# Two linear-attention blocks on one core: other places on the load queue for eight of ten form loads of M

## The chip, the cores and the metric

The kernel runs on one core of a Trainium2 chip. The metric is device time in microseconds for one execution, as the median of several runs. Before the change it is 567.69 us (3 runs, 566.89 to 568.5).

## The reference

Two independent blocks, A and B, of linear attention stand side by side; their outputs are joined on the last axis. Each has 2048 tokens (S), width 640 (D), 32 heads of 20:

```
qkv = (x @ wqkv) -> q, k, v per head
phi(t) = where(t > 0, t + 1, exp(t)) + 1e-6
kv = sum over s of phi(k)[s] (x) v[s]      # 20 x 20 per head
z  = sum over s of phi(k)[s]
o  = (phi(q) @ kv) / (phi(q) . z + 1e-6)
out = concat_heads(o) @ wo
```

All in float32.

## The kernel before, in words

Every matrix product in float32 precision is made of three products of a rounded high part and a remainder (`h` and `l` at the end of a name): high by high, high by low, low by high. ScalarE rounds to the high part, VectorE subtracts to get the low part.

The work falls into two halves.

*The k half* (to about 280 us) goes through both blocks' tokens. It computes phi(k) and the 640 x 640 matrix of x^T phi(k) (`gacc`). From `gacc` and the weights of v the products kv are made, and from kv and `wo` the matrix M = diag(kv) wo of 640 x 640, so that the output is (phi(q) / denominator) M. In this half a planner (class `Plan`) orders the instructions: each step is a note with an engine, a cost, and the parts of tiles it reads and writes. The low parts of x^T are written to DRAM (`xd`, one buffer for each unit of 512 tokens) and so are the ten forms of block A's M (`fd`): sums and differences of M's blocks, from which the last product is made with fewer multiplications. Each form is a pair, high and low, of 128 x 640 (320 KB each; forms 6, 7 and 9 are 128 x 320).

*The q half* goes by units of 512 tokens, 0 to 3 of block A and 4 to 7 of block B. Unit u has five columns c of 128 features. `qmm` makes a column of q with 15 matmuls of 128 x 512 (L1015 to L1017): five row blocks k, three products each. The moving operands are `xqh` (rounded by ScalarE at L1053 from the raw load `xqs`) and `xql` (the low part, loaded from `xd`). For column 0 of units 0 and 1 the order differs: first the ten products with `xqh` (L1153, L1154), then the five with `xql` (L1159). `qphi` takes exponential and relu on ScalarE and joins them on VectorE; `qacc` sums the denominator; `split_acc`, `denmm` (the matmuls `psd`, L1193 and L1194), `recip` and `divide` finish it for unit 0 during unit 1. Then `outmm(0)` makes the output of unit 0 with the forms `fh`, `fl` (0 to 5) and `fm`, `fl` (6 to 9), L1313. It follows unit 1's columns. Its products read forms 0 and 1, then 2 and 3, then 4, 5 and 8, then 6, 7 and 9.

In the q half the order is written by hand: `at(slot, f, ...)` hangs a step on a slot, `("q", u, c, k)` after the matmuls of row block k, or `("o", u, s)` after step s of the output. Slots fix the order in which each engine and each queue gets its instructions; the engines run ahead of each other as far as their waits allow. The loads go out on SP's queue, M's stores of block B and the output on POOL's. SP's transfers take eight semaphores in turn (DMAHW0 to DMAHW7), and one that takes a semaphore anew waits until the transfer that had it before has landed: at most eight are under way.

The steps that the change touches:

- `form_load(b, i)` issues two loads on SP, for the high and the low part of form i (L1140).
- `load_xraw` loads the raw x^T of a unit, five loads of 256 KB (`xqs`, L1046), `load_xq` the low parts, five of 256 KB (`xql`, L1050). Unit 1's first raw load hangs on `("q", 0, 0, 1)`, the other four on `("q", 0, 2, 2)`, its `xql` on `("q", 0, 3, 3)` and after.
- `mmm2(1, i)` makes a third of block B's M: 16 small matmuls (`psm`, L615), four copies by ScalarE (`mev`, L1076). `store_m` issues two stores to `md` on POOL (L1082); six calls make twelve stores, of 60 or 40 rows of 640.
- `load_wo` loads a group's rows of `wo` in two pieces (L631), for the planner through `mmm` (a note with cost 0.14 on SP) and for block B through `load_o`.

Of the kernel before, what the change touches and what calls it, by code (L numbers as in the profile page):

```python
# [15 lines left out]
DH = 20  # L16
# [61 lines left out]
class Plan:  # L78
# [9 lines left out]
    def note(self, engine, n, fn, w, r, ahead=None, dma=None, late=None, by=None, due=None, safe=0.0, lat=0.0):  # L88
        base = self.RATE.get(engine)
        j = Job(engine, base[0] + base[1] * n if base else n, fn, ahead, dma)  # L90
        for part, writes in [(p, True) for p in w] + [(p, False) for p in r]:
            sp = part.space
            if sp.where is not None and sp not in j.spaces:
                j.spaces.append(sp)
            for lo, hi, other, wrote in sp.uses:
                if lo < part.hi and part.lo < hi and (writes or wrote) and other is not j:
                    j.deps.add(other)
            if writes:
                sp.uses = [u for u in sp.uses if not (part.lo <= u[0] and u[1] <= part.hi and u[2] is not j)]
            sp.uses.append((part.lo, part.hi, j, writes))  # L100
        for d in j.deps:
            d.nexts.append(j)
        for sp in j.spaces:
            sp.left += 1
        if engine == "PE":
            j.ideal = self.pe_at
            self.pe_at += j.cost
        j.late = self.pe_at + (25.0 if late is None else late)
        if by is not None:
            j.late = self.pe_at + by  # L110
        j.by, j.set, j.safe, j.lat = by, due, safe, (LAT if due is None else 1.9) + lat
        self.jobs.append(j)
        return j
# [105 lines left out]
def tile_linear_attn_pair(ctx: ExitStack, tc: tile.TileContext, ins, out: bass.AP):  # L219
    nc = tc.nc  # L220
# [60 lines left out]
    note = plan.note  # L281
# [329 lines left out]
    def m_products(o, i, wo, hs):  # L611

        for p in (0, 64):
            for j in range(2):
                nc.tensor.matmul(o[p // 64][j * 64:j * 64 + 64, :HF],  # L615
                                 kvt[p:p + 64, 2 * i + j], wo[j][p:p + 64, hs], start=True, stop=True)

    def m_rows(b, i, a):

        rows = md[b].rearrange("(d h) n -> d h n", h=H)  # L620
        out = []
        for j in range(2):
            h0, nh = GROUPS[2 * i + j]
            n = nh // 2
            out.append((rows[:, h0 + a * n:h0 + a * n + n, :], slice(j * 64, j * 64 + DH * n)))
        return out

    def load_wo(eng, to, b, g):
        h0, nh = GROUPS[g]
        for p, row in ((0, h0 * DH), (64, (h0 + nh) * DH - 64)):  # L630
            eng.dma_start(to[p:p + 64], ins[b]["wo"][row:row + 64, :])  # L631

    def kvmm(k):
        ws = []
# [13 lines left out]
    def mmm(i):  # L648
        n = gn[0] - (3 if i % 2 else 4)
        ks = ((3, 4, 5)[n % 3], (3, 4, 5)[(n + 1) % 3], 6, 7)  # L650
        wo, m = ([Space(n, D, ANY) for _ in range(2)] for n in ("wo", "mev"))
        for j in range(2):
            note("SP", 0.14, lambda j=j: load_wo(nc.sync, wo[j].all.f, 0, 2 * i + j), [wo[j].all], [], ahead=14.0, dma=1.0)

        def products():
            for h in range(2):
                o = [BK[k].open("psm") for k in ks[2 * h:2 * h + 2]]
                m_products(o, i, [x.all.f for x in wo], slice(h * HF, h * HF + HF))

        note("PE", 1.3, products, [BK[k].all for k in ks], [x.all for x in wo] + [KVT.all])  # L660
        for h in range(2):
            hs = slice(h * HF, h * HF + HF)
            for a in range(2):
                k = ks[2 * h + a]
                note("ACT", HF, lambda a=a, k=k, hs=hs: act(m[a].all.f[:, hs], BK[k].tile[:, :HF], AF.Copy), [m[a][hs]],
                     [BK[k].all])
        for a in range(2):
            for j, (rows, part) in enumerate(m_rows(0, i, a)):
                w = 4 * i + 2 * a + j
                note("SP", 0.07, lambda a=a, rows=rows, part=part: nc.sync.dma_start(rows, m[a].all.f[part]),  # L670
                     [mdv[w:w + 1]], [m[a].all], dma=0.5)
# [87 lines left out]
    a, z, x = jh[0][0:P], jl[0][0:P], jr[0][0:P]  # L759
# [127 lines left out]
    for p in range(4, NPB):  # L887
        i, h = divmod(p - 2, 2)
# [9 lines left out]
    for p in range(NPB + 1, NP):  # L898
        if p == NPB + 1:
            fl = kvs  # L900
        else:
            i, h = divmod(p - NPB - 2, 2)
            gready(NG + i)
            fl = filled(NG + i, h, p in (NPB + 2, NP - 1))
        for (q, n), i in place.items():
            if q == p - NPB:
                fl.setdefault(n, []).append((mmm, i))
        kpair(p, fl)
        if p == NPB + 4:
            zsums(0)  # L910
        if p == NPB + 5:
            m_forms()
# [8 lines left out]
    j = note("HOST", 0.0, swap, [gate.all], [])  # L921
# [50 lines left out]
    for g, (h0, nh) in enumerate(GROUPS):  # L972
        cols = NC * DH * nh
        w = Space("wv", cols, (BD,))
# [46 lines left out]
    def at(slot, f, *a):  # L1021
        todo.setdefault(slot, []).append((f, a))
# [34 lines left out]
    def load_o(b, g):  # L1057
        tag = ("dsh0", "dsl0", "dsh1", "dsl1", "dah1", "dal1")[g]
        o = q2[0].tile([P, D], F32, name="wo", tag=tag, bufs=1)
        load_wo(nc.sync, o, b, g)  # L1060
        wot[b, g] = o
# [309 lines left out]
            at(a, form_split, b, i)  # L1371
            at(s, form_store, b, i)

    for i in range(6):
        at((("q", 0, 2, 1), ("q", 0, 2, 4), ("q", 0, 3, 1), ("q", 1, 0, 0), ("q", 1, 0, 2), ("q", 1, 1, 0))[i],
           form_load, 0, i)
    for i in range(6, 10):
        at(("q", 1, i - 5, 4) if i < 9 else ("q", 1, 4, 0), form_load, 0, i)

    for g in range(NGR):  # L1380
        at(("q", 0, 0, 0), load_o, 1, g)
# [1 line left out]
    for i in range(3):  # L1383
        at((("q", 0, 3, 1), ("q", 0, 4, 0), ("q", 0, 4, 4))[i], mmm2, 1, i)
        for h in range(2):
            at((("q", 0, 3, 3), ("q", 0, 3, 4), ("q", 0, 4, 2), ("q", 0, 4, 3), ("q", 1, 0, 1), ("q", 1, 0, 3))[2 * i + h],
               store_m, nc.gpsimd)

    for c, a in ((0, ("q", 1, 4, 1)), (2, ("q", 1, 4, 1)), (4, ("q", 2, 0, 3)), (1, ("q", 4, 0, 2)), (3, ("q", 4, 0, 2))):
# [11 lines left out]
    h = NG - 1  # L1401
# [26 lines left out]
    for v in range(1, NU):  # L1428
        w, u = v - 1, v + 1
# [8 lines left out]
        else:  # L1438
            a = (5, 6, 7, 8, 8, 10, 11) if v == 1 else (2, 3, 5, 6, 7, 9, 11)
# [75 lines left out]
```

## Time and profile before

| What | Before |
|---|---|
| median of 3 runs | 567.69 us (566.89 to 568.5) |
| the profiled execution | 569.47 us |
| its span, first to last instruction | 567.7 us |
| TensorE busy (PE) | 557.9 us, 98% |
| VectorE (DVE) | 414.3 us, 73% |
| ScalarE (ACT) | 351.5 us, 62% |
| POOL | 74.6 us, 13% |
| moved by DMA | 119.60 MB, mean 211 GB/s |
| mean granted TensorE clock | 0.994 |

Busy times are unions of the instructions' spans. Matmuls are pipelined, so that one that takes 0.39 us starts 0.23 us after the one before. Where rows name an idle time in brackets, the arrow points to what ended it. Times within the span count from its first instruction. The execution's own time is 1.77 us longer than the span.

### The profile page before, as it was taken

What the parts mean: (1) busy time and instruction counts of PE and PEld (TensorE: products, weight loads), DVE (VectorE), ACT (ScalarE), POOL (GpSimd) and SP (SyncE); (2) the same over time, 40 slices, a digit from 0 to 9 for tenths busy, and PEclk for the clock granted to TensorE, in tenths of its full rate; (3) what the DMA queues carried; (4) which work ended last, traced back from release to release, by engine and by line L of the source; (5) the groups of instructions that cost most, each with busy time, mean ns of one, the idle gap of its engine ahead of it and who ended that gap; (6) DMA issues with size and microseconds to landing.
All of it is one profiled execution on the core that took longest, in us unless ns stands there. A gap on an engine that the chain in (4) does not pass through costs nothing.

```text
span 567.7 us, 9238 instructions
## 1 busy us (share of the span) xinstructions
PE 557.9 (98%) x3368; PEld 501.2 (88%) x3368; DVE 414.3 (73%) x657; ACT 351.5 (62%) x644; POOL 74.6 (13%) x127
## 2 busy tenths in 40 slices
PE   8999999999999999999999799999999999999997
PEld 6999999989998899998885589898989989898997
DVE  7788687589987668887632499967788686767792
ACT  6777475574768647676227268775767666665551
POOL 1210111111113001111215003110012201001010
PEclk9999999999999999999999799999999999999999
DMA  8994765849869577897999965763363997122022
GB/s 313 377 259 117 184 166 114 270 110 312 257 136 268 185 191 225 240 273 212 353 282 326 373 236 164 272 218 120 107 241 124 346 389 262 48 75 92 1 94 92
DMA packets 69509, 119.60 MB, mean 211 GB/s; under 512 B 7320, under 2 KB 30776, under 8 KB 69464
## 3 DMA queue, kind: packets, MB, share of 16 engines
q1 hardware_dynamic: 59576, 90.39, 48.0%
q0 software_dynamic: 9600, 28.23, 18.0%
q8 instruction: 26, 0.43, 0.3%
q10 hardware_dynamic: 288, 0.39, 0.3%
q14 instruction: 19, 0.16, 0.1%
HBM read 72.44 MB, written 36.07 MB: 191 GB/s over the span
## 4 chain that ended last, share of the span: by engine, by line
PE 93%; DMA 4%; DVE 2%; issue 0%; ACT 0%; SPq 0%; DVEq 0%; ACTq 0%
PE psg L547 19%; PE pa L1313 12%; PE ka L315 10%; PE psq L1015 7%; PE psq L1016 7%; PE psq L1017 7%; PE pe L1313 6%; PE ke L315 5%; PE psr L547 5%; PE psk L812 4%; PE psb L1313 4%; PE kb L315 3%; DMA xql<-xd 2%; PE pskv L602 1%; DMA xqs<-in_A_xt 1%; PE psm L615 1%
## 5 line engine op out<-in xcount | busy, mean ns | idle before, releaser
L1015 PE MATMUL psq<-xqh,wh 128*128 128x512 f32 x190 | 74.8, 394 | 0.0
L1017 PE MATMUL psq<-xqh,wl 128*128 128x512 f32 x190 | 74.6, 393 | 0.0
L1016 PE MATMUL psq<-xql,wh 128*128 128x512 f32 x190 | 74.5, 392 | 0.0
L547 PE MATMUL psg<-pkh,xnl 128*128 128x512 f32 x160 | 63.0, 394 | 0.0
L547 PE MATMUL psg<-pkl,xnh 128*128 128x512 f32 x160 | 63.0, 393 | 0.0
L547 PE MATMUL psg<-pkh,xnh 128*128 128x512 f32 x160 | 62.4, 390 | 0.0
L1173 DVE SCALAR_TENSOR_TENSOR pq<-eq,rq 128x512 f32<-128x512 f32 x40 | 27.6, 691 | 44.2 <-ACT rq L1172 44.2
L1171 ACT ACTIVATE eq<-psq 128x512 f32<-128x512 f32 x40 | 24.0, 600 | 55.3 <-PE psq L1017 44.7
L493 ACT ACTIVATE kt<-ka 128x320 f32<-128x320 f32 x52 | 22.6, 435 | 56.3 <-PE ka L315 56.1
L410 POOL DMA_DIRECT2D zacc<-ek x32 | 26.2, 819 | 198.2 <-DVE ek L503 164.8
L1328 ACT ACTIVATE o<-pa 128x320 f32<-128x320 f32 x64 | 27.9, 438 | 26.2 <-PE pa L1313 25.5
L1015 PEld LDWEIGHTS psq<-xqh,wh 128*128 128x128 f32 x190 | 36.0, 189 | 8.3 <-issue 1.0
L1017 PEld LDWEIGHTS psq<-xqh,wl 128*128 128x128 f32 x190 | 36.0, 189 | 7.7
L1016 PEld LDWEIGHTS psq<-xql,wh 128*128 128x128 f32 x190 | 36.0, 189 | 7.3
L547 PEld LDWEIGHTS psg<-pkh,xnl 128*128 128x128 f32 x160 | 30.0, 188 | 6.5
L547 PEld LDWEIGHTS psg<-pkh,xnh 128*128 128x128 f32 x160 | 30.1, 188 | 4.9
L547 PEld LDWEIGHTS psg<-pkl,xnh 128*128 128x128 f32 x160 | 30.0, 188 | 4.8
L503 DVE SCALAR_TENSOR_TENSOR ek<-ek,kt 128x640 f32<-128x640 f32 x26 | 21.4, 821 | 16.2 <-ACT kt L502 16.2
L405 ACT ACTIVATE pkh<-ek,epst 128x640 fp32r<-128x640 f32 x32 | 26.4, 827 | 5.7 <-DVE ek L503 5.7
L406 DVE SCALAR_TENSOR_TENSOR pkl<-ek,pkh 128x640 fp32r<-128x640 f32 x32 | 26.2, 820 | 3.7 <-ACT pkh L405 3.7
L560 DVE TENSOR_TENSOR gacc<-psg,gacc 128x512 f32<-128x512 f32 x30 | 20.5, 688 | 11.6 <-PE psg L547 11.3
L309 DVE TENSOR_TENSOR xnl<-xns,xnh 128x640 fp32r<-128x640 f32 x32 | 25.6, 819 | 0.8 <-ACT xnh L306 0.8
(225 smaller groups left out, 1638.4 us busy)
## 6 DMA issues: line engine op xcount, KB each, us to landing
zacc<-ek POOLq DMA_DIRECT2D x32, 320.0 KB, 4.6
xql<-xd SPq DMA_DIRECT2D x40, 256.0 KB, 5.7
xd<-xl SPq DMA_DIRECT2D x29, 320.0 KB, 4.0
out<-o POOLq DMA_DIRECT2D x28, 320.0 KB, 3.9
xns<-in_A_x SPq DMA_DIRECT2D x16, 320.0 KB, 4.6
xts<-in_B_xt_tiles SPq DMA_DIRECT2D x16, 320.0 KB, 4.4
xns<-in_B_x SPq DMA_DIRECT2D x16, 320.0 KB, 5.8
xqs<-in_A_xt SPq DMA_DIRECT2D x20, 256.0 KB, 6.2
```

The source lines that it names most:

```text
L309: note("DVE", n, lambda: tt(lo.r, src.f, hi.f, op=OP.subtract), [lo], [src, hi], ahead=10.0)
L315: nc.tensor.matmul(o, a.r, w.r, start=start and k == i == 0, stop=k == n - 1 and i == 2, skip_group_check=True)
L405: note("ACT", n + 110, lambda: act(hi.r, p.f, AF.Identity, bias=epst), [hi], [p, K0.all], by=8.0)
L406: note("DVE", n, lambda: stt(lo.r, p.f, EPS, hi.f, op0=OP.add, op1=OP.subtract), [lo], [p, hi], by=9.0)
L410: note("POOL", 1.0, lambda: nc.gpsimd.dma_start(z.f, p.f, **kw), [z], [p], dma=1.0 if first else 1.86)
L547: nc.tensor.matmul(o[:, :n], a.r, w.r, start=j == 0 and q == 0, stop=j == 2 and q == 2, skip_group_check=True)
L1015: nc.tensor.matmul(o, whi, xhi, start=first, stop=False)
L1016: nc.tensor.matmul(o, whi, xlo, start=False, stop=False)
L1017: nc.tensor.matmul(o, wlo, xhi, start=False, stop=last)
L1173: nc.vector.scalar_tensor_tensor(pq[u][:, c, :], e, 1.0, r, op0=OP.min, op1=OP.add)
L1313: nc.tensor.matmul(ps, x, y, start=start and n == i == 0, stop=n == len(terms) - 1 and i == 2, skip_group_check=True)
L1328: copy = lambda x, y: nc.scalar.activation(x, y, AF.Copy)
```

## The change

Three edits. The loads of the ten forms of block A hang on other slots: forms 0 and 1 in unit 0 ahead of the four raw loads of unit 1's x^T, the other eight in unit 1, with 8 ahead of 6 and 7. The last four of the six `store_m` calls hang on slots of unit 1, where two did. `load_wo` cuts the group's rows out of `wo` first, and its note costs 0.07.

```
     def load_wo(eng, to, b, g):
         h0, nh = GROUPS[g]
-        for p, row in ((0, h0 * DH), (64, (h0 + nh) * DH - 64)):
-            eng.dma_start(to[p:p + 64], ins[b]["wo"][row:row + 64, :])
+        w = ins[b]["wo"][h0 * DH:(h0 + nh) * DH, :]
+        for p, row in ((0, 0), (64, nh * DH - 64)):
+            eng.dma_start(to[p:p + 64], w[row:row + 64, :])
...
-            note("SP", 0.14, lambda j=j: load_wo(nc.sync, wo[j].all.f, 0, 2 * i + j), [wo[j].all], [], ahead=14.0, dma=1.0)
+            note("SP", 0.07, lambda j=j: load_wo(nc.sync, wo[j].all.f, 0, 2 * i + j), [wo[j].all], [], ahead=14.0, dma=1.0)
...
-    for i in range(6):
-        at((("q", 0, 2, 1), ("q", 0, 2, 4), ("q", 0, 3, 1), ("q", 1, 0, 0), ("q", 1, 0, 2), ("q", 1, 1, 0))[i],
-           form_load, 0, i)
-    for i in range(6, 10):
-        at(("q", 1, i - 5, 4) if i < 9 else ("q", 1, 4, 0), form_load, 0, i)
+    for i, a in ((0, ("q", 0, 1, 0)), (1, ("q", 0, 1, 3)), (2, ("q", 1, 0, 1)), (3, ("q", 1, 0, 4)), (4, ("q", 1, 1, 1)),
+                 (5, ("q", 1, 1, 4)), (8, ("q", 1, 2, 1)), (6, ("q", 1, 2, 4)), (7, ("q", 1, 3, 1)), (9, ("q", 1, 4, 0))):
+        at(a, form_load, 0, i)
...
-            at((("q", 0, 3, 3), ("q", 0, 3, 4), ("q", 0, 4, 2), ("q", 0, 4, 3), ("q", 1, 0, 1), ("q", 1, 0, 3))[2 * i + h],
+            at((("q", 0, 4, 2), ("q", 0, 4, 3), ("q", 1, 0, 3), ("q", 1, 0, 4), ("q", 1, 1, 2), ("q", 1, 1, 3))[2 * i + h],
                store_m, nc.gpsimd)
```

After the change line numbers from `load_wo` to the table of the form loads are one higher, and behind that table one lower. On SP's queue, at the end of unit 0, there stand before (`xqs` is raw x^T, `fh` and `fl` a form's two parts with the form's number in `fdh01` and the like, `xql` the low part of x^T, here of unit 1):

```order
L1046 DMA xqs_3451<-in_A_xt 128x512
L1140 DMA fh_3501<-fdh00_100 128x640
L1140 DMA fl_3502<-fdl00_101 128x640
L1046 DMA xqs_3571<-in_A_xt 128x512
L1046 DMA xqs_3573<-in_A_xt 128x512
L1046 DMA xqs_3575<-in_A_xt 128x512
L1046 DMA xqs_3577<-in_A_xt 128x512
L1140 DMA fh_3585<-fdh01_102 128x640
L1140 DMA fl_3586<-fdl01_103 128x640
L1140 DMA fh_3602<-fdh02_104 128x640
L1140 DMA fl_3603<-fdl02_105 128x640
L1050 DMA xql_3633<-xd1_87 128x512
```

and after the change, in the same place:

```order
L1047 DMA xqs_3451<-in_A_xt 128x512
L1141 DMA fh_3476<-fdh00_100 128x640
L1141 DMA fl_3477<-fdl00_101 128x640
L1141 DMA fh_3489<-fdh01_102 128x640
L1141 DMA fl_3490<-fdl01_103 128x640
L1047 DMA xqs_3575<-in_A_xt 128x512
L1047 DMA xqs_3577<-in_A_xt 128x512
L1047 DMA xqs_3579<-in_A_xt 128x512
L1047 DMA xqs_3581<-in_A_xt 128x512
L1051 DMA xql_3627<-xd1_87 128x512
```

Form 1's pair moved ahead of four raw loads, and form 2's pair moved from ahead of the five `xql` to behind them. Further on SP's queue, in unit 1, the narrow forms stand before like this (`xqs` is now unit 2's; in `fm` lie forms 6 to 9):

```order
L1140 DMA fm_3790<-fdh06_114 128x320
L1140 DMA fm_3790<-fdl06_115 128x320
L1140 DMA fm_3790<-fdh07_116 128x320
L1140 DMA fm_3790<-fdl07_117 128x320
L1046 DMA xqs_3838<-in_A_xt 128x512
L1046 DMA xqs_3843<-in_A_xt 128x512
L1046 DMA xqs_3852<-in_A_xt 128x512
L1046 DMA xqs_3857<-in_A_xt 128x512
L1140 DMA fm_3790<-fdh08_112 128x640
L1140 DMA fm_3790<-fdl08_113 128x640
L1046 DMA xqs_3864<-in_A_xt 128x512
```

and after it like this:

```order
L1141 DMA fm_3807<-fdh08_112 128x640
L1141 DMA fm_3807<-fdl08_113 128x640
L1141 DMA fm_3807<-fdh06_114 128x320
L1141 DMA fm_3807<-fdl06_115 128x320
L1047 DMA xqs_3838<-in_A_xt 128x512
L1141 DMA fm_3807<-fdh07_116 128x320
L1141 DMA fm_3807<-fdl07_117 128x320
L1047 DMA xqs_3845<-in_A_xt 128x512
L1047 DMA xqs_3854<-in_A_xt 128x512
L1047 DMA xqs_3859<-in_A_xt 128x512
L1047 DMA xqs_3864<-in_A_xt 128x512
```

Form 8 moved ahead of 6 and 7 and of unit 2's raw loads; from form 9 on the queue is the same in both. On POOL's queue the stores of M (`md`) stand before between the sums of z (`zq`) and the stores of block B's forms (`fdh`, `fdl`):

```order
L688 DMA zq<-zd_95 32x4x5 x4
L1082 DMA md_99<-mev 20x3x640 x8
L1082 DMA md_99<-mev 20x2x640 x4
L1121 DMA fdh_4042<-fsh 128x640
L1121 DMA fdl_4043<-fsl 128x640
```

and after the change:

```order
L689 DMA zq<-zd_95 32x4x5 x4
L1083 DMA md_99<-mev 20x3x640 x8
L1083 DMA md_99<-mev 20x2x640 x4
L1122 DMA fdh_4042<-fsh 128x640
L1122 DMA fdl_4043<-fsl 128x640
```

Here nothing moved but the line numbers.

## Prediction

> **What bounds the kernel now.** First the chain that ended last, by engine (the page's part 4), then in order of time:
> ```profile
> PE 93%; DMA 4%; DVE 2%; issue 0%; ACT 0%; SPq 0%; DVEq 0%; ACTq 0%
> ...
> 300.51 6.17 DMA xqs<-in_A_xt
> 306.75 10.28 DMA xql<-xd
> ```
> TensorE carries 93% of the chain, and an edit of loads gains nothing there. Of the 4% of DMA the larger part, 16.5 us, is one place: the raw x^T of unit 1 and behind it the low parts of x^T (`xql`). So this place was read next. TensorE's timeline there (start, length, operation; in brackets the idle time before it):
> ```profile
> 310.89 0.39 PE L1154 MATMUL psq<-xqh,wl 128*128 128x512 f32 x1
> 314.76 0.63 PE L1159 MATMUL psq<-xql,wh 128*128 128x512 f32 x1 [3.48 <-DMA xql<-xd]
> 315.62 0.79 PE L1159 MATMUL psq<-xql,wh 128*128 128x512 f32 x1 [0.23 <-DMA xql<-xd]
> 317.07 1.93 PE L1159 MATMUL psq<-xql,wh 128*128 128x512 f32 x3 [0.66 <-DMA xql<-xd]
> 318.80 0.63 PE L1015 MATMUL psq<-xqh,wh 128*128 128x512 f32 x1
> ...
> 321.79 0.41 PE L1194 MATMUL psd<-ac,same 128*128 128x512 f32 x1
> 322.04 0.40 PE L1015 MATMUL psq<-xqh,wh 128*128 128x512 f32 x1
> 322.27 0.39 PE L1016 MATMUL psq<-xql,wh 128*128 128x512 f32 x1
> ```
> At full pace a matmul starts every 0.23 us (322.04 to 322.27). The first column of unit 1 does its ten products with `xqh` and then needs the five `xql` (L1159): it waits 3.48 us for the first and goes on as they land. Without a wait the column's end would be 310.89 + 6 x 0.23 = 312.27, and 322.04, fourteen matmuls on, would be 314.1: some 7.9 us are lost here. The windows of this stretch say how (after the length stand the busy times of TensorE, its weight loads, VectorE, ScalarE and POOL, then granted clock, DMA share, GB/s):
> ```profile
> 311.12:314.76 3.64, 0.16 (x2) 0.00 (x1) 2.13 (x3) 0.73 (x2) 1.16 (x2) 1.00 1.04 404
> 314.76:318.80 4.04, 3.15 (x5) 1.54 (x6) 0.00 (x0) 0.00 (x0) 0.00 (x0) 0.53 1.03 404
> 318.80:322.04 3.24, 3.24 (x10) 2.51 (x8) 0.69 (x1) 1.90 (x3) 0.00 (x0) 0.54 1.06 394
> ```
> The wire is full (share 1.03 and more) while TensorE waits, and after the wait TensorE runs at half clock until about 321.8. So two things are lost: time until the last `xql` lands, and then nine matmuls at half pace. What stands ahead of `xql` on SP's queue shows in its timeline:
> ```profile
> 296.85 0.54 SPq L1046 DMA_DIRECT2D xqs<-in_A_xt  x1
> 297.44 0.42 SPq L1140 DMA_DIRECT2D fh<-fdh  x1
> 297.91 0.43 SPq L1140 DMA_DIRECT2D fl<-fdl  x1
> 298.44 2.94 SPq L1046 DMA_DIRECT2D xqs<-in_A_xt  x4
> 301.43 0.42 SPq L1140 DMA_DIRECT2D fh<-fdh  x1
> 301.90 0.42 SPq L1140 DMA_DIRECT2D fl<-fdl  x1
> 302.43 0.48 SPq L1140 DMA_DIRECT2D fh<-fdh  x1
> 303.25 0.39 SPq L1140 DMA_DIRECT2D fl<-fdl  x1
> 303.89 5.38 SPq L1050 DMA_DIRECT2D xql<-xd  x5
> 310.42 0.32 SPq L1140 DMA_DIRECT2D fh<-fdh  x1
> 312.07 0.32 SPq L1140 DMA_DIRECT2D fl<-fdl  x1
> 313.71 0.32 SPq L1140 DMA_DIRECT2D fh<-fdh  x1
> 314.73 0.32 SPq L1140 DMA_DIRECT2D fl<-fdl  x1
> ...
> 318.18 0.32 SPq L1140 DMA_DIRECT2D fm<-fdl  x1
> ```
> SP's transfers use eight semaphores in turn, so from 310.42 on each issue tells that the transfer eight places before it has landed: form 1's `fl` at 310.42, form 2's `fh` at 312.07 and `fl` at 313.71, the first `xql` at 314.73 (TensorE starts at 314.76), the last at 318.18. They land in the order of the queue.
>
> **The change, part by part.** Form 2's pair (2 x 320 KB = 0.655 MB) leaves the place ahead of `xql`. What that is worth hangs on who else uses the wire. DMA queues of 310.4 to 313.7, when that pair landed, then q1 (SP) of 313.7 to 318.2, then the wire of 317 to 321, when SP had it alone:
> ```profile
> q1 hardware_dynamic: 408, 0.79, 61.8%
> q0 software_dynamic: 233, 0.55, 42.2%
> ...
> q1 hardware_dynamic: 722, 1.45, 82.9%
> ...
> DMA packets 715, 1.61 MB, mean 402 GB/s; under 512 B 79, under 2 KB 87, under 8 KB 715
> ```
> The other user is POOL (q0) with M's twelve stores. At the least, `xql` comes earlier by the pair's bytes on a free wire, 0.655 / 0.402 = 1.6 us; at the most by all the time between form 1's and form 2's landings, 313.71 - 310.42 = 3.3 us. SP's own rate up to the last `xql`, 1.45 MB in 4.5 us, gives 0.655 / 0.322 = 2.0 us, and this I take as the base, being the rate of the very transfers that move.
>
> [...]
>
> Form 1's pair is put ahead of the four raw loads of unit 1 (`xqs`), which so land some 2.0 us later (1.6 to 3.3 by the same rows). ScalarE rounds them in its order:
> ```profile
> 306.77 0.63 ACT L1053 ACTIVATE xqh<-xqs 128x512 fp32r<-128x512 f32 x1 [0.18 <-DMA xqs<-in_A_xt]
> 308.31 1.43 ACT L1076 ACTIVATE mev<-psm 128x320 f32<-128x320 f32 x4 [0.91 <-PE psm L615]
> 309.60 0.66 ACT L1053 ACTIVATE xqh<-xqs 128x512 fp32r<-128x512 f32 x1
> ...
> 313.43 0.69 DVE L1006 TENSOR_TENSOR ac<-acc,ac 128x512 fp32r<-128x512 f32 x1 [0.70 <-ACT ac L1009]
> ```
> The rounding at 306.77 waited for its load already, so it goes to about 308.8; behind it on ScalarE stand the last four copies of M (to 309.4 to 310.8), the last rounding (to 311.5) and the exponential of unit 0's last column. TensorE, which used that last rounding before 310.89, waits about 1 us for it and ends its ten products at 312.1. That costs nothing while the first `xql` lands later, at 314.7 - 2.3 = 312.4; without that cover it would cost the 1 us. The exponential is 1.4 us later, and so is VectorE's low part of the denominator, at 314.12 now, then 315.5; TensorE wants it at about 317.5. Covered too. One gain follows: the last four of M's stores start 1.1 us later, and for that time SP has the 17% of the wire that q1's 82.9% left: 0.17 x 0.402 x 1.1 = 0.08 MB, 0.25 us. Shift 2.3 us, last `xql` at 315.9.
>
> Then the clock. In the new order TensorE does two matmuls at 311.6 to 312.1 and five between 312.4 and 315.9, a landing about every 0.9 us, where it now stands still for 3.48 us in one piece. I take it that the clock stays full. From the last landing to the place of 322.04 it then needs 9 x 0.23 = 2.1 us and not 322.04 - 318.18 = 3.9: 1.8 us more. Beyond that place VectorE's reciprocals start where they did, relative to TensorE, within 0.1 us. That leaves 2.3 + 1.8 - 0.1 = 4.0 us.
>
> [...]
>
> The eight pairs in unit 1: their bytes are the same, so the wire is done with them when it is now. The pair of form 2 is read first, and late:
> ```profile
> 325.64 0.65 SPq L1140 DMA_DIRECT2D fl<-fdl  x1
> ...
> 338.09 0.41 PE L1313 MATMUL pa<-fh,dsh 128*128 128x320 f32 x1
> ```
> That read stands at 338.09 now and at 334 then; form 2 follows `xql` on the queue and lands by 318. The last pair, issued at 325.64 now as then, lands some 6 us later and is read last, after 336. Cover of 5 us and more: nothing. Form 8 goes before 6 and 7, which is the order of reading: nothing.
>
> M's stores: POOL issues its transfers in a row of its own, whose rows the calls don't move, and each waits for ScalarE's copies only. Nothing, but for the copies' delay above. `load_wo` slices differently and issues the same two transfers. Its planner cost of 0.07 moves no row on any engine; it gives some tiles other slots, and with them other waits, such as one of SP's x load for POOL's sum:
> ```profile
> 178.02 0.85 POOL L410 DMA_DIRECT2D zacc<-ek  x1 [0.29 <-DVE ek L503]
> ...
> 206.33 0.94 SPq L302 DMA_DIRECT2D xts<-in_B_xt_tiles  x2
> ```
> POOL's transfer goes out 28 us before the load that now waits for it: nothing.
>
> Sum: the profiled execution's 569.47 (its span 567.7) would become 565.5. The runs' median, 567.69, stands 1.78 below that execution; I take the 4.0 from it too: **563.7 us**. Under 0.3%, 1.7 us, a measurement of this kernel can't tell from no change.
>
> **The rivals.** *Only the shift counts.* Half clock comes again, because the stretch from 311 to 316 holds seven matmuls, 1.6 us of work in 5; or the timed runs have none to lose: 1.78 us, by which they lie below the profiled execution, is just the clock's price. For it: clock 0.53 with TensorE busy 3.15 of 4.04 us, so partial work didn't release it at once. Against: the drop came after one whole gap. Time: 567.7 - 2.3 = 565.4. [...]
>
> *No change.* The wire freed goes to M's stores first, and the last `xql` gains under 1 us. For it: q0 had up to 42.2%. Against: the row of 317 to 321 has SP alone, so those stores have ended before the last `xql` anyway and 1.6 us are left even then, unless the raw loads, which come later now, keep the wire badly used. Time: about 567.
>
> *Slower.* The half clock begins later, at the column's end. Now it lasts from about 315.0 to 321.8, 6.8 us, of which over three lie in the wait. If all of it fell on running matmuls it would cost 3.4 us, 1.6 more than now. It decides if the shift is under 1.6 us; with a shift of 0.4, 568.9.
>
> That the change doesn't do what it says holds for a part: the stores of M stay where they are.
>
> **How the numbers follow.** Forecast 0.55, only the shift 0.27, no change 0.13, slower 0.05. The forecast's own range is a shift of 1.6 to 3.3 us with the clock's 1.8, less 0.1: 562.7 to 564.4; only the shift: 564.4 to 566.1. With some 0.3 of scatter 562.4 to 566.4 leaves out the other two, 0.18. Faster 0.82 (the first two), the same 0.13, slower 0.05.
>
> **What would show it.** In the changed kernel: `xql` landing by 316; TensorE's idle gap before the first of them under 2 us; granted clock 1.00 from 311 to 322; rounding of unit 1's raw x^T 1.5 to 2 us later; no wait for `fh`, `fl` or `fm` at the first output; M's stores in the same row on POOL, the last four 1 us later. Wrong would be: `xql` landing at 317 or after, a clock of 0.5 in that place, or a new wait for forms from 334 on.

## The result, and the profile after

| | Before | After |
|---|---|---|
| median of the runs taken together | 567.72 us (7 runs, 566.89 to 568.64) | 564.52 us (7 runs, 562.86 to 565.79) |
| ratio, with 95% interval | | 0.9939 (0.9921 to 0.9957) |
| the profiled execution, its span | 569.47 us, 567.7 us | 565.79 us, 564.0 us |
| mean granted TensorE clock in it | 0.994 | 0.997 |

The change makes the kernel faster by 3.2 us, 0.6%. The forecast was 563.7 us, with a range of 562.4 to 566.4; the median lies 0.8 us above the forecast.

The chain of the profiled execution after, by engine, misleads at first sight: DMA's share has grown from 4% to 9%.

```profile
PE 89%; DMA 9%; DVE 0%; ACT 0%; issue 0%; SPq 0%; ACTq 0%
...
305.03 8.38 DMA xql<-xd
...
326.46 5.63 DMA xql<-xd
```

The chain now follows SP's queue through unit 1, while TensorE works beside it. What TensorE lost stands in the table of its waits; here its first row before the change and its first after (in all, times, longest):

```profile
PE psq L1159 <- DMA xql<-xd: 4.4, 3, 3.5
```

```profile
PE psq L1160 <- DMA xql<-xd: 1.8, 3, 1.0
```

TensorE's timeline after the change, at the place shown in the prediction (line numbers are one higher):

```profile
310.73 0.39 PE L1155 MATMUL psq<-xqh,wl 128*128 128x512 f32 x1
310.95 0.40 PE L1160 MATMUL psq<-xql,wh 128*128 128x512 f32 x1
311.99 0.49 PE L1160 MATMUL psq<-xql,wh 128*128 128x512 f32 x1 [0.64 <-DMA xql<-xd]
313.44 1.09 PE L1160 MATMUL psq<-xql,wh 128*128 128x512 f32 x2 [0.96 <-DMA xql<-xd]
314.70 0.80 PE L1160 MATMUL psq<-xql,wh 128*128 128x512 f32 x1 [0.16 <-DMA xql<-xd]
...
318.33 0.39 PE L1016 MATMUL psq<-xqh,wh 128*128 128x512 f32 x1
```

The first `xql` is there when it is wanted, and the gap of 3.48 us has become gaps of 0.64, 0.96 and 0.16 us. The matmul that stood at 322.04 stands at 318.33: 3.71 us, and the span is 3.7 us shorter. So everything was gained here and nothing lost later. SP's timeline shows the landings (an issue tells that the transfer eight places before has landed: TensorE starts on an `xql` at 311.99, 313.44 and 314.70, 0.02 to 0.03 us behind the issues at 311.96, 313.42 and 314.67):

```profile
299.28 2.40 SPq L1047 DMA_DIRECT2D xqs<-in_A_xt  x4
302.08 4.71 SPq L1051 DMA_DIRECT2D xql<-xd  x5
...
310.56 0.32 SPq L1141 DMA_DIRECT2D fl<-fdl  x1
...
314.67 0.32 SPq L1141 DMA_DIRECT2D fl<-fdl  x1
```

The five `xql` land at 310.56 to 314.67; before, at 314.73 to 318.18. Of ScalarE three rows matter:

```profile
306.44 2.07 ACT L1054 ACTIVATE xqh<-xqs 128x512 fp32r<-128x512 f32 x3 [1.16 <-DMA xqs<-in_A_xt]
308.42 1.40 ACT L1077 ACTIVATE mev<-psm 128x320 f32<-128x320 f32 x4
309.69 0.65 ACT L1054 ACTIVATE xqh<-xqs 128x512 fp32r<-128x512 f32 x1
```

The three roundings of raw x^T end at 308.51, where they ended at 307.40 before: 1.1 us later. But the copies of M and the last rounding come 0.1 us later, not a microsecond. TensorE's row at the first output has no wait for a form. The clock, in three stretches of 3.41 us (columns as in the prediction's windows):

```profile
311.05:314.46 3.41, 1.72 (x5) 0.56 (x3) 2.14 (x3) 0.89 (x2) 1.10 (x2) 1.00 1.05 411
314.46:317.87 3.41, 3.25 (x9) 2.50 (x9) 0.69 (x1) 1.52 (x3) 0.00 (x0) 0.50 1.03 407
317.87:321.28 3.41, 3.41 (x16) 2.82 (x15) 2.74 (x2) 1.02 (x3) 0.00 (x0) 1.00 1.04 395
```

In this execution the clock did not stay full: one stretch of 3.41 us ran at half pace. Before there were two, one behind the other:

```profile
314.97:318.39 3.42, 2.53 (x5) 1.04 (x5) 0.00 (x0) 0.00 (x0) 0.00 (x0) 0.50 1.05 410
318.39:321.80 3.41, 3.41 (x9) 2.64 (x10) 0.69 (x1) 1.90 (x3) 0.00 (x0) 0.50 1.06 397
```

By an estimate from these rows one such stretch takes 0.003 off the mean clock of a run (half of 3.41 us in 564). So the clock of each timed run is read here as the number of its stretches, though not their place: 0.994 two (as in the profiled execution before), 0.997 one (as in the one after), 1.00 none. Of the changed kernel's seven runs four had none (562.86 to 564.52 us, clock 0.999 or 1.00) and three had one (565.13 to 565.79).

### The profile page after: what moved, and what is told of

The parts are those of the page before. It is cut to its first block, busy times and chain, and to the rows that moved or that the text cites. A ratio compares the mean times of both kernels' runs of the same rounds, so it can differ in the third digit from the quotient of the medians.

```text
span 564.0 us, 9238 instructions
## 1 busy us (share of the span) xinstructions
PE 556.6 (99%) x3368; PEld 500.5 (89%) x3368; DVE 414.1 (73%) x657; ACT 351.2 (62%) x644; POOL 74.6 (13%) x127
## 4 chain that ended last, share of the span: by engine, by line
PE 89%; DMA 9%; DVE 0%; ACT 0%; issue 0%; SPq 0%; ACTq 0%
PE psg L547 17%; PE pa L1314 12%; PE ka L315 10%; PE psq L1016 7%; PE psq L1017 7%; PE psq L1018 7%; PE pe L1314 6%; PE ke L315 5%; DMA xql<-xd 5%; PE psr L547 4%; PE psk L813 4%; PE psb L1314 4%; PE kb L315 3%; PE pskv L602 1%; DMA fl<-fdl 1%; DMA xqs<-in_A_xt 1%
## 5 line engine op out<-in xcount | busy, mean ns | idle before, releaser
L1016 PE MATMUL psq<-xqh,wh 128*128 128x512 f32 x190 | 74.8, 394 | 0.0
L1016 PEld LDWEIGHTS psq<-xqh,wh 128*128 128x128 f32 x190 | 36.0, 189 | 8.2 <-issue 1.0
```

The lines of the kernel that those rows point to most:

```text
L1016: nc.tensor.matmul(o, whi, xhi, start=first, stop=False)
```

## The experiments

Theory A: the gain is form 2's pair out of the way of `xql`, on a wire that is shared with M's stores, and a clock that falls less. Rivals: B, it is mostly the clock, which needs the landings broken up; C, other parts of the change carry it (form 1's place, the store slots, `load_wo`). All ratios are to the kernel before, run beside: its medians were 568.39 us (with the first four kernels), 568.16 (the next three) and 568.61 (the last four).

### One slot: form 2's pair behind xql

```
-        at((("q", 0, 2, 1), ("q", 0, 2, 4), ("q", 0, 3, 1), ("q", 1, 0, 0), ...)[i],
+        at((("q", 0, 2, 1), ("q", 0, 2, 4), ("q", 1, 0, 0), ("q", 1, 0, 0), ...)[i],
```

> The kernel before with one slot changed: form 2's pair goes behind the low parts of x^T on SP's queue; form 1's place, the late forms and M's stores stay as before. Theory A (the pair's bytes stood in the way of xql): last xql 1.6 to 3.5 us earlier than in the kernel before, time 564 to 565.5, so all of the gain or nearly all. Theory B (the gain is the clock's, which needs the landings broken up as in the changed kernel): the same time if the clock stays full, 566 if only the landings move. Theory C (form 1 ahead of the raw loads, the late forms' slots or load_wo's slice carry a good part): over 566.

Measured: 565.03 us, ratio 0.9947 (0.9927 to 0.9967): the change's own ratio, within both intervals. Its timeline is that of the changed kernel, nearly to the tenth:

```profile
312.12 0.50 PE L1159 MATMUL psq<-xql,wh 128*128 128x512 f32 x1 [0.16 <-DMA xql<-xd]
313.58 1.14 PE L1159 MATMUL psq<-xql,wh 128*128 128x512 f32 x2 [0.96 <-DMA xql<-xd]
314.93 0.50 PE L1159 MATMUL psq<-xql,wh 128*128 128x512 f32 x1 [0.21 <-DMA xql<-xd]
```

One of ten forms carries the gain, as far as the measurement can tell. Its runs kept a full clock less often than the changed kernel's, 3 of 12 against 10 of 16; whether the rest of the change has a part in that, these runs don't settle.

### One slot: form 1's pair ahead of the raw loads

```
-        at((("q", 0, 2, 1), ("q", 0, 2, 4), ("q", 0, 3, 1), ...)[i],
+        at((("q", 0, 2, 1), ("q", 0, 2, 1), ("q", 0, 3, 1), ...)[i],
```

> The kernel before with one slot changed: form 1's pair goes ahead of unit 1's four raw loads; form 2 stays ahead of xql. Theory A: the same bytes stand ahead of xql, so the last xql lands within 0.5 us of the kernel before's, the rounding of raw x^T comes up to 2 us later and is covered by the wait: 567.7, within 0.3%. Theory C: 565 to 566.5, as a part of the gain would be here; if the late rounding costs, 568 to 569.

Measured: 567.68 us, ratio 0.9996 (0.9979 to 1.0013). No part of the gain is here. TensorE does wait for the late rounding, and then for `xql` all the same:

```profile
310.76 0.50 PE L1153 MATMUL psq<-xqh,wh 128*128 128x512 f32 x1 [0.73 <-ACT xqh L1053]
...
312.77 0.50 PE L1159 MATMUL psq<-xql,wh 128*128 128x512 f32 x1 [1.27 <-DMA xql<-xd]
313.44 2.16 PE L1159 MATMUL psq<-xql,wh 128*128 128x512 f32 x3 [0.17 <-DMA xql<-xd]
315.88 0.80 PE L1159 MATMUL psq<-xql,wh 128*128 128x512 f32 x1 [0.28 <-DMA xql<-xd]
```

The 0.73 us lie under the wait, as forecast. But the last `xql` lands at 315.85 here, 2.3 us ahead of the profiled execution of before, though the same bytes stand ahead of it: more than the 0.5 us expected. The landing moves from execution to execution, and that of before shown in the prediction was a late one.

### Only the store slots and load_wo

The changed kernel with the form table of the kernel before.

> The changed kernel with the form loads' slots of the kernel before: only the store slots and load_wo's slice and planner cost are left of the change. Theory A: POOL's row is the same and nothing reads the cost in this place: 567.7, within 0.3%. Theory C: under 566.5.

Measured: 568.16 us, ratio 0.9994 (0.9974 to 1.0013): nothing, as expected. Of theory C there remain the slots of forms 3 to 9, which no run tests by themselves; the first experiment leaves little for them.

### All forms behind xql

```
-    for i, a in ((0, ("q", 0, 1, 0)), (1, ("q", 0, 1, 3)), (2, ("q", 1, 0, 1)), ...
+    for i, a in ((0, ("q", 0, 4, 4)), (1, ("q", 0, 4, 4)), (2, ("q", 1, 0, 1)), ...
```

> The changed kernel with forms 0 and 1 behind xql too, so that none of the ten forms is ahead of unit 1's x^T. Theory A: each pair ahead is worth its time on the wire until the wait is gone: two pairs, 1.31 MB, 3.3 us or more, of which the wait that is left in the changed kernel can give back some 2.5 us and the half clock 1.2 more: 561 to 562. Theory B (what was to be had was the clock's): 563.5 to 564.5, the changed kernel's time with its clock full. Theory C in another form (the wait moves to the first output, whose form 0 and 1 are then late): a wait for fh or fl at the outputs, time 564.5 or above.

Measured: 563.27 us, ratio 0.9915 (0.9886 to 0.9945), all six runs at a clock of 0.999 or 1.00. Its median lies below the changed kernel's, though the intervals overlap, and above the 561 to 562 expected. TensorE's timeline shows what was gained and lost:

```profile
312.67 0.50 PE L1160 MATMUL psq<-xql,wh 128*128 128x512 f32 x1 [1.00 <-DMA xql<-xd]
...
339.09 0.56 PE L1314 MATMUL pa<-fm,dah 128*128 128x320 f32 x2 [0.87 <-ACT o L1329]
```

Only the last `xql` is waited for. A new wait stands at the first output. It is not a wait for forms but for ScalarE's copy, and ScalarE's and VectorE's timelines lead back to M's rows, loaded again (`wst`):

```profile
336.01 0.74 ACT L1010 ACTIVATE fsh<-wst 128x640 fp32r<-128x640 f32 x1 [0.71 <-DVE wst L1092]
```

```profile
334.95 0.49 DVE L1091 TENSOR_TENSOR t<-wst 128x320 f32<-128x320 f32 x1 [1.20 <-DMA wst<-md]
```

VectorE waits 1.20 us for that load, ScalarE's rounding stands behind VectorE's sum, ScalarE's copy of the output behind the rounding (and behind a second wait for VectorE), TensorE behind the copy. TensorE's place of 322.04 stands at 314.88 here, seven microseconds earlier than before. But that alone doesn't make the load late. In the kernel with form 0 alone ahead (below) this place comes at 314.77, and nothing waits there for `wst`. SP's rows of `wst`, first with all forms behind, then with form 0 ahead, and VectorE's sum in the latter:

```profile
328.74 0.79 SPq L1036 DMA_DIRECT2D wst<-md  x2
```

```profile
326.78 0.79 SPq L1036 DMA_DIRECT2D wst<-md  x2
...
333.57 0.49 DVE L1091 TENSOR_TENSOR t<-wst 128x320 f32<-128x320 f32 x1
```

Forms 0 and 1, put behind `xql`, are themselves ahead of `wst`, which goes out 2.0 us later than with form 0 left in front. With all forms behind, a load further down the queue is late in its turn.

### M's stores on SP, behind xql

```
-            at((("q", 0, 4, 2), ("q", 0, 4, 3), ("q", 1, 0, 3), ...)[2 * i + h], store_m, nc.gpsimd)
+            at((("q", 1, 2, 1), ("q", 1, 2, 1), ("q", 1, 2, 2), ...)[2 * i + h], store_m, nc.sync)
```

> The changed kernel with M's twelve stores on SP's queue behind xql in the third tile of unit 1, instead of on POOL's queue: while xql is under way nothing else uses the wire. Theory A (the wire is shared with those stores, and form 0's and 1's pairs are ahead): POOL's share of the wire of some 30 to 50% goes to SP, last xql about 2 us earlier, time 562 to 563. Rival (the row on SP is paced by its issues or by its own bytes, and what POOL stores fits between): the last xql within 0.5 us of the changed kernel's, time 564 to 565; or the stores, waiting on SP for ScalarE's copies or used late, hold up what stands behind them: slower than 564.5.

Measured: 567.72 us, ratio 0.9989 (0.9974 to 1.0004): as slow as before, yet its first column doesn't wait at all. DMA queues of 304 to 312 us, in this kernel and then in the changed one:

```profile
q1 hardware_dynamic: 1645, 3.16, 104.9%
```

```profile
q1 hardware_dynamic: 1031, 1.88, 65.1%
q0 software_dynamic: 479, 1.15, 36.3%
```

Behind each queue stand its packets, its MB and the time of its packets as a share of the 16 engines' span; q1 is SP's, q0 POOL's. The wire moves some 3.1 MB either way; SP gets all of it or 62%. TensorE's and SP's timelines, and TensorE's next wait:

```profile
310.80 1.35 PE L1160 MATMUL psq<-xql,wh 128*128 128x512 f32 x5
...
342.11 0.90 PE L1314 MATMUL pa<-fm,dah 128*128 128x320 f32 x2 [4.13 <-ACT o L1329]
```

```profile
311.63 0.32 SPq L1141 DMA_DIRECT2D fl<-fdl  x1
...
314.16 10.90 SPq L1083 DMA_DIRECT2D md<-mev  x12
...
331.87 1.01 SPq L1036 DMA_DIRECT2D wst<-md  x2
```

The last `xql` has landed at 311.63, 3.0 us earlier than in the changed kernel (314.67). But the twelve stores occupy SP from 314.16 to 325.1, the `wst` loads behind them go out at 331.87 where the changed kernel had them at 327.16, and the path by VectorE and ScalarE just described holds TensorE up for 4.13 us. Behind that wait TensorE runs at a lower pace. The page's clock is 0.7 in the slice of 340.0 to 354.2 us; on the chain the 18 matmuls from 342.11 take 5.10 us, and the next 18, from 347.21, take 2.65. So M's stores cost `xql` some 3 us of wire, and on SP's queue they cost more later, the wait and 2.45 us of lower pace. Theory and rival were each half right: the shift came, and what stood behind the stores took it back.

### Added matmuls in the wait of the kernel before

```
+        for _ in range(16 if u == 1 and late else 0):
+            nc.tensor.matmul(den[0], zero, zero.unsqueeze(1).to_broadcast([P, 4, P]), start=True, stop=True)
         for k in range(NC if late else 0):
```

> The kernel before with 16 added matmuls on zeros (128 x 512, into a bank that is overwritten later) where TensorE waits 3.48 us for xql: the wait is filled, no byte moves, nothing is left out. Theory A (the shift of the landings is most of the gain, the clock some 1.8 us at the most): landings as before, clock full, last L1159 still at xql's last landing; 565.9 to 566.5. Theory B (the clock is most of it): 564.5 or less. If the price of the half clock is nothing in this place: 567.7.

Measured: 567.26 us, ratio 0.9980 (0.9966 to 0.9994). Seven of the twelve runs had a full clock, median 566.68; five had one stretch at half pace, median 568.56. The median of all lies above the 565.9 to 566.5 of theory A, which took the clock to be full in every run. In the profiled one the clock is full behind the filled gap, and the landings are where they were (last `xql` at 317.3):

```profile
311.28:314.70 3.42, 3.42 (x18) 1.65 (x17) 2.14 (x3) 0.73 (x2) 0.95 (x2) 1.00 1.05 405
314.70:318.10 3.40, 2.15 (x8) 1.24 (x8) 0.00 (x0) 0.14 (x1) 0.00 (x0) 1.00 1.02 399
```

So with the landings unmoved the clock gives 568.2 - 566.7 = 1.5 us where it stays full and 0.9 in the median, where the change gave 3.2. As a cause by itself theory B falls; the clock is a part.

### Added matmuls in the changed kernel

First four, ahead of its five late products:

```
+        for _ in range(4 if u == 1 and late else 0):
+            nc.tensor.matmul(den[0], zero, zero.unsqueeze(1).to_broadcast([P, 4, P]), start=True, stop=True)
```

> The changed kernel with 4 added matmuls on zeros in the same place (0.9 us of work): nothing else. If the half clock that the changed kernel still has in some of its runs costs the 2 us by which its runs differ: all runs at a clock of 1.00 and a median of 563 to 563.5. If 4 matmuls don't fill the stretch enough, or the half clock is hidden by the landings: 564.5, as the changed kernel.

Measured: 564.12 us, ratio 0.9938 (0.9917 to 0.9959), the changed kernel's; three of eight runs still had a clock of 0.996 or 0.997 and took 566.3 to 567.5. So four don't keep the clock full in every run. Then two ahead of each of the five products:

```
         for k in range(NC if late else 0):
+            for _ in range(2 if u == 1 else 0):
+                nc.tensor.matmul(den[0], zero, zero.unsqueeze(1).to_broadcast([P, 4, P]), start=True, stop=True)
```

> The changed kernel with ten added matmuls on zeros, two ahead of each of unit 1's five late products of xql, so that 2.3 us of TensorE's idle time are filled and no byte moves. Theory (the changed kernel's median lies between runs with one window at half clock and runs with none): nearly all runs at a clock of 1.00, median 563.3 to 563.8. Rival (the half clock comes from something else than this stretch's idle time, or the added work delays as much as it gives): 564.5 or above, with the same mixture of clocks.

Measured: 563.79 us, ratio 0.9925 (0.9903 to 0.9948), all six runs at 0.999 or 1.00. With the small gaps filled no run shows the half clock, which points to them as its cause. It isn't proof: at the changed kernel's rate, 10 full runs of 16, six full runs in a row would come about one time in seventeen. The changed kernel itself ran beside it:

> The changed kernel itself once more, on the same chip as these, to compare them by: 564.5, some runs at a clock of 0.997 near 565.3 and some at 1.00 near 563.6.

Measured: 564.10 us, ratio 0.9931 (0.9909 to 0.9952); three of nine runs at 0.996 or 0.997 (565.32 to 566.3), six at a full clock (562.54 to 564.37). Without the slower third the median falls by 0.3 us, which is not more than the measurement can tell. The added work has its own price: in the profiled executions, both at a full clock, the next column's first matmul (L1016) starts at 315.35 with the ten added ones and at 314.61 without.

### Form 1 behind xql, form 0 ahead

```
-    for i, a in ((0, ("q", 0, 1, 0)), (1, ("q", 0, 1, 3)), (2, ("q", 1, 0, 1)), ...
+    for i, a in ((0, ("q", 0, 1, 0)), (1, ("q", 0, 4, 4)), (2, ("q", 1, 0, 1)), ...
```

> The changed kernel with form 1 behind xql, so that form 0's pair alone stands ahead: between the changed kernel (two pairs ahead) and the one with none. Theory (each pair has its price on the wire, at most 2 us, as long as a wait is left): 563 to 564, last xql 1 to 2 us earlier than in the changed kernel. Rival (the wire's other work counts, and a pair more or less gives nothing once two are gone): 564.5.

Measured: 562.16 us, ratio 0.9900 (0.9876 to 0.9923): the fastest of all by its median, 1.9 us below the changed kernel run beside it and 6.45 below the kernel before; its interval and the changed kernel's overlap a little. It lies below the 563 to 564 expected. The one wait left is for the last `xql`:

```profile
312.58 0.50 PE L1160 MATMUL psq<-xql,wh 128*128 128x512 f32 x1 [0.77 <-DMA xql<-xd]
```

A pair more behind `xql` brought the last landing from 314.25 (the changed kernel beside it) to 312.56, 1.7 us. With form 0 behind too it came no earlier (312.64, and 313.47 in the kernel of the next experiment). The wire of 300 to 305 us suggests why; first with form 0 ahead, then with all forms behind:

```profile
300.00:305.00 5.00, 5.00 (x33) 3.35 (x32) 1.44 (x2) 3.84 (x10) 2.71 (x5) 1.00 1.02 370
```

```profile
300.00:305.00 5.00, 5.00 (x32) 3.38 (x33) 1.45 (x2) 3.84 (x11) 2.44 (x4) 1.00 0.89 286
```

The wire moved 286 GB/s against 370: form 0's pair seems to fit where the wire would have had room.

### All forms behind, and M's rows loaded earlier

The kernel of "All forms behind xql", with one line more changed:

```
-    for c, a in ((0, ("q", 1, 4, 1)), (2, ("q", 1, 4, 1)), ...
+    for c, a in ((0, ("q", 1, 3, 2)), (2, ("q", 1, 3, 2)), ...
```

> The kernel with no form ahead of xql, and two loads of M's rows (wst) put ahead of three of unit 2's raw loads. Theory (what that kernel still loses at its first outputs, 0.87 us of TensorE's idle time, is ScalarE's row held up by VectorE's sums of the late wst): the wait at the outputs goes, 0.9 to 1.2 us less than without the edit, 562 to 562.5. Rival (the wait at the outputs is the forms', or the raw loads, now later, hold ScalarE's row instead): the wait stays or moves, 563 to 564.

Measured: 562.72 us, ratio 0.9903 (0.9881 to 0.9925), just above the 562 to 562.5 expected. TensorE's wait at the outputs is gone, and ScalarE's rounding of `wst` no longer waits:

```profile
336.01 0.72 ACT L1010 ACTIVATE fsh<-wst 128x640 fp32r<-128x640 f32 x1
```

So the account of that wait is right. The times, 0.55 us apart on different chips, don't tell the two kernels apart.

## Why the prediction was right, point by point

**The place and the part.** Form 2's pair alone gives 0.9947, form 1's place 0.9996, stores and `load_wo` 0.9994. The prediction put nearly the whole gain on the pair and costed the rest at nothing, but for 0.25 us by a delay of M's stores.

**The shift.** Forecast 2.3 us. The two profiled executions differ by 3.5 (318.18 to 314.67), but that is chance of the one before. SP's rows at the last landing tell it for seven more executions. Three of them have three pairs ahead of `xql`, as the kernel before has (form 1 moved, stores only, the filled wait):

```profile
315.85 0.32 SPq L1140 DMA_DIRECT2D fm<-fdl  x1
316.42 0.32 SPq L1141 DMA_DIRECT2D fm<-fdl  x1
317.34 0.32 SPq L1140 DMA_DIRECT2D fm<-fdl  x1
```

Four have two, as the changed kernel has (the changed kernel again, form 2 moved, four and ten added matmuls):

```profile
314.25 0.32 SPq L1141 DMA_DIRECT2D fl<-fdl  x1
314.91 0.32 SPq L1140 DMA_DIRECT2D fl<-fdl  x1
314.49 0.32 SPq L1141 DMA_DIRECT2D fl<-fdl  x1
314.08 0.32 SPq L1141 DMA_DIRECT2D fl<-fdl  x1
```

With 318.18 and 314.67 the means are 316.9 and 314.5. The difference is 2.5 us, and the term was right. So was taking a rate between a free wire (1.6) and all the time between two landings (3.3): from 304 to 312 us of the changed kernel SP had 62% of the two queues' bytes (1.88 of 3.03 MB) and POOL 38%.

In time the shift is less sure. With one stretch at half pace the kernel before took 567.2 us (median of 6 runs), the changed one 565.5 (6 runs): 1.7. With a full clock the kernel before with its wait filled took 566.7 (7 runs), the changed one with four added matmuls 563.8 (5 runs, same chip): 2.9. The kernel before itself kept a full clock in two of the 68 runs beside the experiments, at 563.52 and 565.66; the changed kernel's ten such runs lie at 562.54 to 564.52. Runs picked by their clock may be picked by their landings too, so these times bear the 2.5 us out only roughly.

**The clock.** This term was right in some runs only. The prediction took it that the clock stays full, an assumption that no run had shown, with a chance of 0.55, and had "only the shift" as a rival with 0.27. Both came. In the 16 timed runs of the changed kernel ten had no stretch at half pace, median 563.85 us (forecast 563.7), and six had one, median 565.51 (the rival's 565.4). The median falls in the larger group, near its upper end. In the first seven runs that was four against three: that the forecast came out and not the rival was in part luck. The prediction had named a clock of 0.5 in this place as a sign of being wrong, and the profiled execution shows it. The step that failed is "the drop came after one whole gap": in the profiled execution no gap is over 0.96 us, and the half clock came all the same, after a stretch in which TensorE's row shows 1.72 of 3.41 us. From the last landing to the place of 318.33 that execution took 3.66 us, against 3.86 before: 0.2 us of the 1.8 were gained there. Where the clock stayed full, in the changed kernel's second profile, it took 2.21 (314.25 to 316.46): 1.65 of the 1.8.

Half pace lasted 6.83 us before (314.97 to 321.80) and 3.41 after (314.46 to 317.87), and after it came behind a stretch with TensorE about half busy. How little work brings it, the runs don't settle: stretches of 3.41 us with 1.72 and 2.10 us of work (after, and form 2 moved alone) were followed by half pace, one of 3.40 us with 2.15 (the second row of the filled wait) was not. But where the clock stayed full, no row shows where such a stretch would begin; its place there is the author's choice.

**The rounding of the raw x^T.** Forecast: last four copies of M 1.1 us later, TensorE's last rounding 1 us later, covered. In the profiled execution the roundings ended 1.1 us later and not 2, and the copies behind them came 0.1 us later. The row that the prediction quoted holds the rest of the reason: ahead of those copies ScalarE had 0.91 us of idle time, waiting for TensorE, and the working didn't count it. The four stores behind them began at 309.78 instead of 309.70, so the 0.25 us that SP was to gain from their delay had no ground. In other executions TensorE's wait is there (0.30 us in the changed kernel's second profile, 0.73 with form 1 moved, 0.83 with four added matmuls). The cover held.

**Forms, M's stores, load_wo.** No wait for a form at the first output, in any of these traces. POOL's stores kept their order and their times within 0.7 us. The prediction's cover for the later steps was too narrow in one respect: it named the forms as what could be late in unit 1, and what is late when forms 0 and 1 go behind `xql` too is the `wst` load behind them.

**The slower rival**, half clock later and dearer, didn't come: it needed a shift under 1.6 us.

## What to carry to other kernels

Read the queue ahead of the operand that is waited for: one pair of loads that is needed some 20 us later, standing ahead of it, cost 2.5 us of landing here, and moving one slot gave as much as a table of ten, within what the measurement can tell. Then look at what stands behind the place to which a load is moved: with every form behind `xql`, `wst`, further down the queue, was late. Here a wait for loads was paid for twice: a stretch of 3.41 us in which TensorE's row shows 1.72 us, with no gap over 0.96, was followed by 3.41 us at a clock of 0.50. Before explaining a shift by two profiles, look at the same quantity in more executions: the last landing spread over 2.3 us among kernels with the same bytes ahead of it.

## What was not expected of the hardware

In the profiled execution after, half clock (0.50 from 314.46 to 317.87) came without a single idle gap of TensorE over 0.96 us in the stretch ahead of it. In the kernel before, the second stretch at half pace, 318.39 to 321.80, followed one at half pace in which TensorE's row shows 2.53 of 3.42 us; the clock was 1.00 again only from 321.80, behind the stretch with 3.41 of 3.41. And with M's stores off the wire, the last `xql` landed 3.0 us earlier: a second queue with 36% of the DMA engines' time cost the first about as much as a pair of forms ahead of it did (2.5).
